# Rows of each expert loaded in parts of 16·m partitions, and one load of columns issued from another queue

## The chip, the core and the metric

One core of one Trainium2 chip. The metric is the device time of one execution in microseconds (us); before the change it is 1216.14 us, the median of three runs (1215.63 to 1216.97). Engines are called PE (matmul), PEld (its weight load), DVE (vector), ACT (scalar), POOL (GpSimd) and SP (the engine that here only issues transfers). About 2.4 us, 0.2% of the time, is what a measurement of this kernel can tell from no change.

## The reference

Three layers follow each other: attention that keeps the 32 largest scores of a row, a mixture of eight experts of which each token takes one, and a dense two-layer network.

```python
def _attn_ref(q, k, v):                       # 4 x 8 x 576 x 64
    scores = scale * np.matmul(q, k.transpose(0, 1, 3, 2))
    kth = np.partition(scores, -top_k, axis=-1)[..., -top_k:-top_k + 1]
    scores = np.where(scores >= kth, scores, -1000000000.0)
    ...
def _moe_ref(x, expert_emb, tau, w1, w2):     # 2304 tokens of 512, 8 experts, 1024 hidden
    expert_idx = np.argmax(logits, axis=1)
    for e in range(E):
        mask = expert_idx == e
        h = np.maximum(x[mask] @ w1[e], 0.0)
        out[mask] = gate_w[mask, None] * (h @ w2[e])
def _moe2_ref(x, w_in, w_out, alpha):         # 512 -> 2048 -> 512
    h = x @ w_in
    g = np.maximum(h, 0.0) + alpha * np.minimum(h, 0.0)
    return g @ w_out
```

## The kernel before

The attention runs to about 515 us. While it ends, the router finds the expert of each token and scatters the tokens' rows into the DRAM array `xs`, one region of 2304 rows for each expert; a row has 512 values, the token's number and its gate. The experts are then sorted by their number of tokens. The largest is rank 0, and each rank has a fixed number of columns that it computes: `CAPS`, 472, 408, 360, 328, 304, 296, 280 and 256.

`Experts.run` works on nine blocks: the first 216 tokens of rank 0 (`FIRST`, partly computed ahead, under the attention), its other 256, and ranks 1 to 7. A block of n tokens is a first product and a second product, 96 matmuls each. In the first product (lines 989 to 991) eight hidden tiles are computed, each twelve matmuls of n columns, into one of six PSUM banks (`mm`); ACT takes each out with a Relu (L1082) and DVE computes the low half (L1083). In the second product four output tiles (`dc` 0 to 3) are computed, 24 matmuls each. Tiles 0 and 2 are taken out by DVE (L1127), tiles 1 and 3 by ACT (L1125), into `y`, which has two buffers in all; from there SP stores them to the DRAM array `yt` (L1128), two ticks later. So tile 3 can be taken out only once the store of tile 1 has landed, and tile 2 once that of tile 0 has.

The rows of a block are loaded by `load_rows` (L957) into the tile `xr`, which has one buffer. Such a load is issued in the second product of the block two before, as soon as the rows that stood there have been transposed. A load of n rows is cut into nj parts of p partitions, where nj is the smallest of 1 to 4 that divides n into parts of at most 128: 216 is 2 x 108, 256 is 2 x 128, 408 is 4 x 102, 360 is 3 x 120, 328 is 4 x 82, 304 is 4 x 76, 296 is 4 x 74, 280 is 4 x 70. ACT multiplies each part by the gates (L973), in the first product of the block before the one that the rows are for. PE transposes the rows in four chunks, one matmul for each part and chunk (L981), in the second product of that same block; ACT and DVE take the chunks out (L983, L984). Four ticks after its load, `load_rows` also has the tokens' numbers copied from `xs` to the DRAM list `idc` (L964); for the first block it is done at once and from the tile (L967).

Weights are loaded on SP's queue too (L849 for the experts, L894 for the last network), converted by ACT (L923) and by DVE or POOL (L924), in the order in which `tick` meets them. All engines work in the order in which this code is written; SP's queue has the loads of rows, of weights and the stores of results, one behind the other.

After the experts, `last_products` runs the dense network in groups of 256 tokens. Its columns come back from `yt` through `load_columns` (L1143), again into `xr`. The load of the first group is issued in the second product of rank 6, that of the second group at the start of the first group's products. A rank stores its whole number of columns at a place that is known only at run time, so the framework lets a load from `yt` wait for every store before it, and a store wait for every load before it, unless the two are declared independent.

Of the kernel before, what the change touches and what calls it, by code (L numbers as in the profile page):

```python
# [21 lines left out]
P = 128  # L22
# [408 lines left out]
NT = B * S  # L431
E, FF, FF2, DM = 8, 1024, 2048, H * D
# [14 lines left out]
G2 = 256  # L447
# [367 lines left out]
class Experts:  # L815
# [3 lines left out]
    def __init__(self, tc, w1, w2, w_in, w_out, wa, xp, ident, xs, yt, idc, yp, ro, out):  # L819
        self.tc, self.nc = tc, tc.nc  # L820
        self.w1, self.w2, self.w_in, self.w_out = w1, w2, w_in, w_out
        self.ident, self.xs, self.yt, self.idc, self.out = ident, xs, yt, idc, out
        self.ro, self.wa, self.xp, self.yp = ro, wa, xp, yp
        self.W, self.rv = {}, {}
        self.items, self.sent = [], 0
        self.h0, self.p0 = [], []

    def reg(self, ap, n):
        return self.nc.values_load(ap, engines=[mybir.EngineType.SP], min_val=0, max_val=n,
# [102 lines left out]
    def after(self, n, f):  # L932

        self.stores.append((self.step + n, f))

    def tick(self, at, of):

        self.step += 1
        for x in [x for x in self.stores if x[0] <= self.step]:
            self.stores.remove(x)  # L940
            x[1]()
        k = (at + 1) * self.n // of - at * self.n // of if at >= 0 else 0
        for _ in range(k):
            if self.done == self.sent:
                self.send(1)
            self.items[self.done][1]()
            self.done += 1
            self.send(self.done + 3 - self.sent)

    def load_rows(self, r, o, n):  # L950

        nc = self.nc
        nj = next(j for j in (1, 2, 3, 4) if n % j == 0 and n // j <= P)
        p = n // nj
        e, base = self.rv[r]
        x = self.xp.tile([P, 4, XW], F32, name="xr")
        ld = nc.sync.dma_start(x[:p, :nj], self.xs[ds(e * NT + o, n)].rearrange("(j p) d -> p j d", p=p))  # L957
        if r == 0 and o == 0:
            assert len(self.ro.scat) == (B - 1) * BT
            self.ro.early = ld  # L960
        ids = self.idc[ds(base + o, n)] if r else self.idc[o:o + n]
        if r or o:
            src = self.xs[ds(e * NT + o, n), DM]
            self.after(4, lambda: nc.sync.dma_start(ids.rearrange("(a b) -> a b", a=8),  # L964
                                                    src.rearrange("(a b) -> a b", a=8)))
        else:
            nc.sync.dma_start(ids.rearrange("(j p) -> p j", p=p), x[:p, :nj, DM])  # L967
        return x, p, nj

    def gate(self, rows, j):  # L970
# [67 lines left out]
    def run(self, ctx, alpha):  # L1038
        tc, nc = self.tc, self.nc
        self.wb = ctx.enter_context(tc.tile_pool(name="wb", bufs=1, reuse_waits="tile"))  # L1040
        self.wk = ctx.enter_context(tc.tile_pool(name="moe", bufs=1, reuse_waits="tile"))
        self.ps = ctx.enter_context(tc.tile_pool(name="moe_ps", bufs=1, space=PSUM, reuse_waits="tile"))
        self.V, self.done, self.step, self.stores = {}, 0, 0, []
        blocks = [(0, 0, FIRST), (0, FIRST, CAPS[0] - FIRST)] + [(r, 0, CAPS[r]) for r in range(1, E)]
        units = lambda r, i: [self.plain(k) for k in range(8 * r + 4 * i, 8 * r + 4 * i + 4) if EARLY <= k < 8 * E]

        plan = [units(0, 1), [], units(1, 0), units(1, 1)]
        for r in range(1, E):
            plan += [units(r + 1, 0), units(r + 1, 1)]
        plan[-2] += [self.last(u) for u in range(4)]  # L1050
        plan[-1] += [self.last(u) for u in range(4, 8)]
        plan.append([self.wide(u, i) for u in range(STAY, 16) for i in range(2)])
        wide = [self.wide(u, i) for u in range(STAY) for i in range(2)]
        n = len(wide)
        first, m = WIDE
        for i in range(m):
            p = plan[first + i]
            at = lambda i: i if i == 0 else 4 + (n - 4) * (i - 1) // (m - 1)
            new = wide[at(i):at(i + 1)]
            plan[first + i] = [x for y in zip(p[:len(new)], new) for x in y] + p[len(new):] + new[len(p):]  # L1060
        self.wf = self.wb.tile([P, STAY, 1024], F32, name="wf")
        self.items = [x for p in plan for x in p]
        self.send(4)
        rki = self.ro.rki
        ranks = self.ro.ranks()

        def registers():
            for r in range(1, E):
                self.rv[r] = (self.reg(rki[0:1, 0, r:r + 1], E - 1), self.reg(rki[0:1, 1, r:r + 1], NT))
        self.alpha = self.wk.tile([P, FF2 // P], F32, name="alpha")  # L1070
        nc.sync.dma_start(self.alpha, alpha.rearrange("(f p) -> p f", p=P))
        xT = self.x0
        for i, (r, o, n) in enumerate(blocks):
            nb = blocks[i + 1] if i + 1 < len(blocks) else None
            hT, nx = ([] if i else self.h0), []
            self.n = len(plan[2 * i])
            for f in range(8):
                if i or f >= AHEAD:
                    ps = self.bank()[:, :n]
                    self.hidden(r, f, xT, ps)  # L1080
                    h = self.hidden_tile(f, [P, 2, MAXN])
                    nc.scalar.activation(h[:, 0, :n], ps, AF.Relu)  # L1082
                    nc.vector.scalar_tensor_tensor(h[:, 1, :n], ps, 0.0, h[:, 0, :n].bitcast(F32), op0=OP.max,  # L1083
                                                   op1=OP.subtract)
                    hT.append(h)
                if i == 0:
                    k = RANKS[f]
                    for step in ranks[:k]:
                        step()
                    ranks = ranks[k:]  # L1090
                    if len(ranks) < 14 and 1 not in self.rv:
                        registers()
                        rows = [self.load_rows(*nb)]
                if f >= GAT and nb and i:
                    self.gate(rows[0], f - GAT)
                if i:
                    self.tick(f, 8)
                else:
                    self.tick(SPLIT0.index(f) if f in SPLIT0 else -1, len(SPLIT0))
            if not nb:  # L1100
                nx = self.halves(rows[0])
            if i == 1:
                fl = self.flags()
            if i == 2:
                self.redo(*fl)
            base = self.rv[r][1]
            self.n = len(plan[2 * i + 1])

            def turn(at):
                if nb:  # L1110
                    nx.extend([self.x_chunk(rows[0], nb[2], d) for d in (XAT if i else XAT0)[at]])
                    if len(nx) == 4 and len(rows) == 1:
                        rows.append(self.load_rows(*blocks[i + 2]) if i + 2 < len(blocks) else self.load_columns(0))
            for dc in range(4):
                ps = self.bank()[:, :n]
                for f in range(8):
                    u = self.W[8 * r + 4 + f // 2]
                    c = slice((f % 2) * 512 + dc * P, (f % 2) * 512 + (dc + 1) * P)
                    self.mm3(ps, u[:, 0, c], u[:, 1, c], hT[f][:, 0, :n], hT[f][:, 1, :n], f == 0, f == 7)
                    if f == 3:  # L1120
                        self.tick(2 * dc, 8)
                        turn(2 * dc)
                y = self.wk.tile([P, 512], F32, name="y", bufs=2)
                if dc % 2:
                    nc.scalar.activation(y[:, :n], ps, AF.Copy)  # L1125
                else:
                    nc.vector.tensor_copy(y[:, :n], ps)  # L1127
                self.after(2, lambda r=r, o=o, n=n, dc=dc, y=y, base=base: nc.sync.dma_start(  # L1128
                    self.yt[dc, :, ds(base + o, n)] if r else self.yt[dc, :, o:o + n], y[:, :n]))
                self.tick(2 * dc + 1, 8)  # L1130
                if nb:
                    if i == 0 and dc == GAT0:
                        for j in range(4):
                            self.gate(rows[0], j)
                    turn(2 * dc + 1)
            xT, rows = nx, rows[1:]
        self.last_products(xT, len(plan[-1]))

    def load_columns(self, g):

        x = self.xp.tile([P, 4, XW], F32, name="xr")
        if g * G2 < NT:
            self.nc.sync.dma_start(x[:, :, :G2], self.yt[:, :, g * G2:(g + 1) * G2].rearrange("c p t -> p c t"))  # L1143
        return x

    def halves(self, x):
# [461 lines left out]
```

## Time and profile before

| what | us |
|---|---|
| median of three runs | 1216.14 |
| the profiled execution's own time | 1218.64 |
| its span, first to last instruction | 1216.8 |
| attention and router | 0 to about 525 |
| blocks of the experts | about 525 to 791 |
| dense network | 791 to 1216.8 |
| PE busy in the span | 1171.7 (96%) |

The span is read by stages: PE is at work nearly everywhere, so a change is worth what it gives back of the time in which PE waits, or of the matmuls themselves. The blocks of the experts can be told apart in the trace by the number of columns of their matmuls (128x408, 128x360 and so on), and the first product from the second by what is multiplied (`xT` or `hT`).

### The profile page before, as it was taken

To read this page: it belongs to the slowest core of one execution; us is meant where nothing else is said; L and a number is where in the kernel's file an instruction comes from. 1 tells how busy PE (TensorE), PEld (TensorE's weight loads), DVE (VectorE), ACT (ScalarE), POOL (GpSimd) and SP (SyncE) were. 2 spreads that over 40 slices of the span, in tenths; PEclk is the share of its full clock that TensorE was granted. 3 is DMA by queue.
4 is the path that set the end of the run, shared out by engine and by line. 5 is a ranking of instruction groups with operands and counts; after the bars stand their busy time and mean duration, and the time that the engine had idled before them with its cause. 6 is when DMAs were issued, how large, how long until landed. Compare 5 with 4: busy or idle time off the path is not lost.

```text
span 1216.8 us, 23815 instructions
## 1 busy us (share of the span) xinstructions
PE 1171.7 (96%) x7729; PEld 1028.1 (84%) x7729; DVE 871.8 (72%) x3629; ACT 695.0 (57%) x1495; POOL 725.6 (60%) x684
## 2 busy tenths in 40 slices
PE   7999999999999999998999899989999999999996
PEld 4778788778877886998999899978898998998995
DVE  5999999999999999776545376666657564454440
ACT  5899999999999998834434355422323222122120
POOL 4899988998999888743334255445345352333331
PEclk9999999999999999888999999989999999999998
DMA  5343222322231103168757688442232212212211
GB/s 132 100 114 109 61 53 56 91 62 55 57 91 37 33 13 132 30 159 223 202 160 197 177 241 236 126 113 70 78 113 70 65 58 70 78 62 78 72 43 55
DMA packets 121538, 120.85 MB, mean 99 GB/s; under 512 B 73380, under 2 KB 91300, under 8 KB 121404
## 3 DMA queue, kind: packets, MB, share of 16 engines
q1 hardware_dynamic: 118492, 109.78, 32.5%
q0 software_dynamic: 2912, 9.46, 2.2%
q8 instruction: 63, 1.03, 0.4%
q14 instruction: 71, 0.58, 0.2%
HBM read 84.25 MB, written 33.92 MB: 97 GB/s over the span
## 4 chain that ended last, share of the span: by engine, by line
PE 72%; DVE 12%; DMA 5%; ACT 3%; POOL 3%; issue 3%; SPq 1%; POOLq 0%; ACTq 0%; DVEq 0%
PE mm L990 10%; PE mm L991 10%; PE mm L989 10%; PE po L310 9%; PE s L165 8%; PE mm L1207 6%; PE mm L1206 6%; PE mm L1205 6%; PE pt L289 4%; DMA yt<-y 4%; DVE cand L186 3%; DVE mg L218 2%; DVE w L208 2%; POOL pm L269 2%; PE pt L145 1%
## 5 line engine op out<-in xcount | busy, mean ns | idle before, releaser
L989 PE MATMUL mm<-xT,wt 128*128 128x256 f32 (+7 forms) x852 | 249.2, 292 | 9.4 <-ACT xT L1150 5.5
L990 PE MATMUL mm<-xT,wt 128*128 128x256 f32 (+7 forms) x852 | 249.9, 293 | 4.3 <-DVE xT L984 4.2
L991 PE MATMUL mm<-xT,wt 128*128 128x256 f32 (+7 forms) x852 | 249.2, 292 | 0.0
L186 DVE MAX8 cand<-ss 128x8 f32<-128x82 f32 (+1 forms) x1008 | 231.7, 232 | 14.2 <-ACT ss L176 14.2
L263 POOL TENSOR_TENSOR z<-ss,sg 128x576 f32<-128x576 f32 x143 | 204.9, 1433 | 47.8 <-ACT sg L252 27.4
L310 PEld LDWEIGHTS po<-vt,pT 116*128 116x128 f32 x1440 | 175.8, 192 | 34.2 <-issue 23.9
L269 POOL TENSOR_TENSOR pm<-e,mg 128x576 f32<-128x576 f32 x141 | 199.1, 1412 | 2.7 <-ACT mg L243 2.2
L310 PE MATMUL po<-vt,pT 116*128 116x130 f32 x1440 | 197.2, 283 | 1.2 <-ACT pc L342 1.0
L1190 POOL TENSOR_TENSOR hT<-xr,hT 128x256 fp32r<-128x256 f32 x144 | 106.3, 743 | 153.3 <-ACT hT L1189 145.7
L1189 ACT ACTIVATE hT<-xr 128x256 fp32r<-128x256 f32 x144 | 59.1, 417 | 200.8 <-DVE xr L1186 194.0
L989 PEld LDWEIGHTS mm<-xT,wt 128*128 128x128 f32 x852 | 163.8, 192 | 11.6 <-ACT xT L1150 5.8
L165 PE MATMUL s<-qk 64*128 64x288 f32 x512 | 166.3, 447 | 3.8 <-ACT ss L176 3.2
L990 PEld LDWEIGHTS mm<-xT,wt 128*128 128x128 f32 x852 | 164.1, 193 | 5.4 <-DVE xT L984 4.4
L991 PEld LDWEIGHTS mm<-xT,wt 128*128 128x128 f32 x852 | 164.8, 193 | 0.0
L924 POOL TENSOR_TENSOR wt<-raw,wt 128x1024 fp32r<-128x1024 f32 x29 | 78.0, 2693 | 91.4 <-ACT wt L923 89.4
L1185 DVE TENSOR_SCALAR xr<-mm,alpha 128x256 f32<-128x256 f32 x144 | 69.3, 481 | 85.2 <-PE mm L991 84.3
L165 PEld LDWEIGHTS s<-qk 64*128 64x128 f32 x512 | 89.6, 194 | 43.7 <-issue 12.5
L252 ACT ACTIVATE sg<-ss,w 128x576 f32<-128x576 f32 x144 | 112.6, 782 | 5.2 <-DVE w L199 5.1
L176 ACT ACTIVATE ss<-s 128x576 f32<-128x576 f32 x144 | 94.9, 659 | 30.2 <-PE s L165 29.4
L257 ACT ACTIVATE e<-ss,sm 128x576 f32<-128x576 f32 x144 | 111.7, 776 | 0.0
L289 PE MATMUL pt<-ident,pm 128*116 128x128 f32 x720 | 105.4, 278 | 6.5 <-POOL pm L269 6.4
L208 DVE MAX8 w<-z 128x8 f32<-128x576 f32 x144 | 106.7, 741 | 2.5 <-POOL z L263 2.4
(249 smaller groups left out, 2493.6 us busy)
## 6 DMA issues: line engine op xcount, KB each, us to landing
raw<-in_moe_w SPq DMA_DIRECT2D x60, 512.0 KB
xr<-yt SPq DMA_DIRECT2D x18, 512.0 KB
xs<-zeros SPq DMA_DIRECT2D x8, 1028.0 KB
raw<-in_moe_w_in SPq DMA_DIRECT2D x16, 512.0 KB
raw<-in_moe_w_out SPq DMA_DIRECT2D x16, 512.0 KB
yt<-zeros SPq DMA_DIRECT2D x8, 704.0 KB
rows<-in_q SPq DMA_DIRECT2D x32, 144.0 KB
rows<-in_k SPq DMA_DIRECT2D x32, 144.0 KB
```

The source lines that it names most:

```text
L165: nc.tensor.matmul(s[:, g, :HALF], qs, t["qk"][hs, S + g * HALF:S + (g + 1) * HALF], start=True, stop=True)
L186: blocks.append(lambda i=i: nc.vector.max(A.cand[:, i], A.ss[:, i * BW:(i + 1) * BW if i + 1 < KB else S]))
L208: fin = [lambda: nc.vector.max(C.w[:, 24:32], C.z), lambda: nc.vector.scalar_tensor_tensor(scr, self.vsel, C.c1, C.w[:, 23:32, None].to_br ...
L252: nc.scalar.activation(T.sg, T.ss, AF.Sign, bias=T.w[:, 23:24], scale=-ABOVE, accum_out=T.c1)
L257: nc.scalar.activation(T.e, T.ss, AF.Exp, bias=T.sm[:, 0:1], scale=0.125)
L263: eng.tensor_tensor(T.z, T.ss, T.sg, op=OP.mult)
L269: eng.tensor_tensor(thirds(T.pm[:, :S]), thirds(T.e), T.mg, op=OP.mult)
L289: nc.tensor.transpose(o, T.pm[:, c * CK:(c + 1) * CK], self.ident)
L310: nc.tensor.matmul(po[:, i:i + 2, :], T.pT[:, c], rhs, start=(c == 0), stop=(c == NCK - 1))
L989: nc.tensor.matmul(ps, wh, xh, start=first, stop=False)
L990: nc.tensor.matmul(ps, wh, xl, start=False, stop=False)
L991: nc.tensor.matmul(ps, wl, xh, start=False, stop=last)
```

## The change

Two edits. In `load_rows` the parts have a multiple of 16 partitions: nj is n over 128, rounded up, and p is the smallest multiple of 16 with which nj parts hold n rows. 216 becomes 2 x 112, 408 4 x 112, 360 3 x 128, 328, 304 and 296 3 x 112, 280 3 x 96; 256 stays 2 x 128. The load then reads 8 to 40 rows more than the block has (none for 256), which lie in the same region of `xs`, and whose transposed columns nobody reads. The first block's numbers are stored part by part, two transfers for one, since its last part is not full. In `load_columns` the first call issues on ACT's queue, the others on SP's as before, and that load and the stores of ranks 2 to 7 are declared independent of each other (`put`, `behind`, `ahead_of`): the first 256 columns belong to rank 0.

```diff
--- before.py
+++ after.py
@@ -823,7 +823,7 @@
         self.ro, self.wa, self.xp, self.yp = ro, wa, xp, yp
         self.W, self.rv = {}, {}
         self.items, self.sent = [], 0
-        self.h0, self.p0 = [], []
+        self.h0, self.p0, self.behind, self.ahead_of = [], [], [], []
 
     def reg(self, ap, n):
         return self.nc.values_load(ap, engines=[mybir.EngineType.SP], min_val=0, max_val=n,
@@ -932,6 +932,14 @@
     def after(self, n, f):
 
         self.stores.append((self.step + n, f))
+
+    def put(self, r, st):
+
+
+        if r > 1:
+            self.behind.append(st)
+            for ld in self.ahead_of:
+                self.tc.declare_no_dep(st.ins, ld.ins, reason="columns of other tokens")
 
     def tick(self, at, of):
 
@@ -950,11 +958,11 @@
     def load_rows(self, r, o, n):
 
         nc = self.nc
-        nj = next(j for j in (1, 2, 3, 4) if n % j == 0 and n // j <= P)
-        p = n // nj
+        nj = -(-n // P)
+        p = -(-n // (16 * nj)) * 16
         e, base = self.rv[r]
         x = self.xp.tile([P, 4, XW], F32, name="xr")
-        ld = nc.sync.dma_start(x[:p, :nj], self.xs[ds(e * NT + o, n)].rearrange("(j p) d -> p j d", p=p))
+        ld = nc.sync.dma_start(x[:p, :nj], self.xs[ds(e * NT + o, p * nj)].rearrange("(j p) d -> p j d", p=p))
         if r == 0 and o == 0:
             assert len(self.ro.scat) == (B - 1) * BT
             self.ro.early = ld
@@ -964,7 +972,9 @@
             self.after(4, lambda: nc.sync.dma_start(ids.rearrange("(a b) -> a b", a=8),
                                                     src.rearrange("(a b) -> a b", a=8)))
         else:
-            nc.sync.dma_start(ids.rearrange("(j p) -> p j", p=p), x[:p, :nj, DM])
+            for j in range(nj):
+                m = min(p, n - j * p)
+                nc.sync.dma_start(self.idc[j * p:j * p + m], x[:m, j, DM])
         return x, p, nj
 
     def gate(self, rows, j):
@@ -1125,8 +1135,8 @@
                     nc.scalar.activation(y[:, :n], ps, AF.Copy)
                 else:
                     nc.vector.tensor_copy(y[:, :n], ps)
-                self.after(2, lambda r=r, o=o, n=n, dc=dc, y=y, base=base: nc.sync.dma_start(
-                    self.yt[dc, :, ds(base + o, n)] if r else self.yt[dc, :, o:o + n], y[:, :n]))
+                self.after(2, lambda r=r, o=o, n=n, dc=dc, y=y, base=base: self.put(r, nc.sync.dma_start(
+                    self.yt[dc, :, ds(base + o, n)] if r else self.yt[dc, :, o:o + n], y[:, :n])))
                 self.tick(2 * dc + 1, 8)
                 if nb:
                     if i == 0 and dc == GAT0:
@@ -1140,7 +1150,12 @@
 
         x = self.xp.tile([P, 4, XW], F32, name="xr")
         if g * G2 < NT:
-            self.nc.sync.dma_start(x[:, :, :G2], self.yt[:, :, g * G2:(g + 1) * G2].rearrange("c p t -> p c t"))
+            eng = self.nc.scalar if not self.ahead_of else self.nc.sync
+            ld = eng.dma_start(x[:, :, :G2], self.yt[:, :, g * G2:(g + 1) * G2].rearrange("c p t -> p c t"))
+            if not self.ahead_of:
+                self.ahead_of.append(ld)
+                for st in self.behind:
+                    self.tc.declare_no_dep(ld.ins, st.ins, reason="columns of other tokens")
         return x
 
     def halves(self, x):
```

SP's queue in the second product of rank 1, where the rows of rank 3 are loaded; `xr<-xs` is the load (partitions x parts x values), `yt<-y` the stores of output tiles 0, 1 and 2, `raw` weights. Before:

```order
L1128 DMA yt<-y 128x408
L849 ISA
L849 DMA raw<-in_moe_w 128x2x512
L957 ISA
L957 DMA xr<-xs 82x4x514
L1128 ISA
L1128 DMA yt<-y 128x408
L849 ISA
L849 DMA raw<-in_moe_w 128x1024
```

After:

```order
L1138 DMA yt<-y 128x408
L849 ISA
L849 DMA raw<-in_moe_w 128x2x512
L965 ISA
L965 DMA xr<-xs 112x3x514
L1138 ISA
L1138 DMA yt<-y 128x408
L849 ISA
L849 DMA raw<-in_moe_w 128x1024
```

Nothing moves: the load stands in the same place, with the store of tile 1 right behind it, and has three parts of 112 partitions for four of 82.

ACT's queue in the second product of rank 6, where the first columns for the dense network are loaded; `xT<-xt` takes out the transposed chunks of rank 7, `y<-mm` the output tiles 1 and 3, `hT<-mm` the hidden tiles of rank 7. Before:

```order
L923 ACTIVATE wt<-raw 128x1024 x2
L983 ACTIVATE xT<-xt 128x256 x2
L1125 ACTIVATE y<-mm 128x280
L983 ACTIVATE xT<-xt 128x256 x2
L923 ACTIVATE wt<-raw 128x1024 x2
L1125 ACTIVATE y<-mm 128x280
```

After:

```order
L923 ACTIVATE wt<-raw 128x1024 x2
L993 ACTIVATE xT<-xt 128x256 x2
L1135 ACTIVATE y<-mm 128x280
L993 ACTIVATE xT<-xt 128x256 x2
L1154 DMA xr<-yt 128x4x256
L923 ACTIVATE wt<-raw 128x1024 x2
L1135 ACTIVATE y<-mm 128x280
```

The load stands on ACT between the last chunks of rank 7 and two weight conversions. On SP, at the same place, it is gone from between a weight load and the store of tile 1. Before:

```order
L849 DMA raw<-in_moe_w 128x2x512
L1143 DMA xr<-yt 128x4x256
L1128 ISA
L1128 DMA yt<-y 128x280
L1128 ISA
```

After:

```order
L849 DMA raw<-in_moe_w 128x2x512
L1138 ISA
L1138 DMA yt<-y 128x280
L1138 ISA
L1138 DMA yt<-y 128x280
```

The stores of tiles 1 and 2 of rank 6 no longer stand behind a load; the order of the others is as it was. On ACT four multiplications by the gates are gone (one part less in ranks 3 to 6), and on PE sixteen transposes.

## Rows read from the trace of the kernel before

**Rows 1.** The page, part 1: busy us, share of the span, instructions.
```profile
PE 1171.7 (96%) x7729; PEld 1028.1 (84%) x7729; DVE 871.8 (72%) x3629; ACT 695.0 (57%) x1495; POOL 725.6 (60%) x684
```

**Rows 2.** Waits of PE from 500 us on: waiting <- releaser, us, times, longest.
```profile
PE mm L989 <- ACT xT L1150: 5.5, 1, 5.5
PE mm L990 <- DVE xT L984: 4.2, 1, 4.2
PE mm L989 <- ACT y L1125: 3.2, 2, 3.0
```

**Rows 3.** PE by stage: stretch, us, busy (instructions), granted clock, DMA share, GB/s.
```profile
596.20:615.37 19.17, 19.17 (x110) 1.00 0.41 136
615.37:632.30 16.93, 16.32 (x97) 1.00 0.70 171
632.30:650.75 18.45, 17.21 (x113) 1.00 0.83 241
650.75:665.25 14.50, 14.50 (x98) 1.00 0.62 167
665.25:681.50 16.25, 15.79 (x114) 1.00 0.60 198
681.50:700.02 18.52, 15.28 (x98) 0.91 0.67 150
700.02:715.51 15.49, 14.81 (x114) 1.00 0.76 246
...
728.53:742.71 14.18, 14.18 (x115) 1.00 0.81 277
...
768.33:779.63 11.30, 11.30 (x98) 1.00 0.17 55
694.40:697.80 3.40, 3.12 (x13) 0.50 0.40 120
```

**Rows 4.** Timeline of ACT, output tile 3: start, us, form, [idle before <- releaser].
```profile
625.04 0.51 ACT L1125 ACTIVATE y<-mm 128x408 f32<-128x408 f32 x1 [15.83 <-DMA yt<-y]
657.57 0.47 ACT L1125 ACTIVATE y<-mm 128x360 f32<-128x360 f32 x1 [12.00 <-DMA yt<-y]
692.50 0.45 ACT L1125 ACTIVATE y<-mm 128x328 f32<-128x328 f32 x1 [15.54 <-DMA yt<-y]
718.05 0.42 ACT L1125 ACTIVATE y<-mm 128x304 f32<-128x304 f32 x1 [5.70 <-DMA yt<-y]
742.95 0.42 ACT L1125 ACTIVATE y<-mm 128x296 f32<-128x296 f32 x1 [3.38 <-PE mm L991]
```

**Rows 5.** The chain that ended last, from 600 us: start, us, what.
```profile
607.11 17.82 DMA yt<-y
```

**Rows 6.** Timeline of SP: start, us taken by issuing.
```profile
675.38 6.84 SPq L1128 DMA_DIRECT2D yt<-y  x1
```

**Rows 7.** Transposes on PE by shape, 535:765 us: count, busy us, mean ns.
```profile
L981 PE MATMUL xt<-ident,xr 102*128 102x102 f32 x16 | 1.7, 250 | 0.0
L981 PE MATMUL xt<-ident,xr 120*128 120x120 f32 x12 | 1.6, 265 | 0.0
L981 PE MATMUL xt<-ident,xr 82*128 82x82 f32 x16 | 1.5, 234 | 0.0
```

**Rows 8.** Timelines of SP (first column load) and of ACT behind it.
```profile
765.64 0.38 SPq L1143 DMA_DIRECT2D xr<-yt  x1
...
771.42 0.40 ACT L1125 ACTIVATE y<-mm 128x280 f32<-128x280 f32 x1 [5.10 <-PE mm L991]
```

**Rows 9.** Waits of SP's queue from 760 to 772 us: us, times, longest.
```profile
SPq L1128 <- DMA xr<-yt: 3.3, 1, 3.3
SPq L1143 <- DMA yt<-y: 3.0, 1, 3.0
```

**Rows 10.** Timeline at the second group's columns: ACT takes them, PE goes on.
```profile
807.73 1.32 ACT L1150 ACTIVATE xT<-xr 128x256 fp32r<-128x256 f32 x4
...
808.18 0.58 PE L989 MATMUL mm<-xT,wt 128*128 128x256 f32 x1 [5.54 <-ACT xT L1150]
```

## The prediction

> **What bounds the kernel now.** I read four views, from the whole to the part. The page's first lines [rows 1] show PE at work for 96% of the span, so what the change can give back lies in the remaining 4% or in the matmuls. PE's waits from 500 us on [rows 2] come to few: 5.5 us for `xT` of the dense network, 4.2 us for an `xT` of the first blocks, 3.2 us for ACT's `y`, and some smaller ones behind DVE. The busy times by stage [rows 3] place the third. The product stages of the experts run at a steady price for each column where nothing disturbs them: in a first product 14.50 us for 328 columns and 11.30 us for 256, both 0.0441 us a column; in a second product, transposes included, 19.17 us for 408 and 14.18 us for 296, that is 0.0470 and 0.0479, middle 0.0474. Against these prices five stages are too long:
>
> - 615.37, rank 2 first, 360 columns: 16.93 against 15.88, 1.05 us over
> - 632.30, rank 2 second, 360: 18.45 against 17.08, 1.37 over
> - 665.25, rank 3 second, 328: 16.25 against 15.56, 0.69 over
> - 681.50, rank 4 first, 304: 18.52 against 13.41, 5.11 over
> - 700.02, rank 4 second, 304: 15.49 against 14.42, 1.07 over
>
> Together 9.3 us. Part of the 5.11 is the clock: after PE had waited, the granted clock was 0.50, the lower level of 1.2 GHz, from 694.40 to 697.80 [rows 3], where 13 matmuls ran in 3.40 us instead of some 24 (13.41 us over 96 is 0.14 us each), a loss of 1.5 us.
>
> The cause stands on ACT [rows 4]. Before it can take out output tile 3, ACT waits for the store of tile 1, since `y` has two buffers: 15.83 us in the stage from 615.37, 12.00 us in that from 650.75, 15.54 us in that from 681.50. While ACT stands there, PE fills the free banks and then stops. The chain that ended last runs through the store: 17.82 us from issue to landing [rows 5]. In front of that store SP had issued the rows of the rank two further on, in four parts of 82 partitions; in the other two long waits they had 76 and 74. Where the load in front had parts of 70, the wait is 5.70 us, and where they were 128 ACT waits for PE instead [rows 4]; the stage between these two, 728.53, is busy throughout [rows 3]. A store took 6.84 us only to be issued [rows 6], so the queue behind such a load was full. The size doesn't sort the waits (4 x 74 rows are fewer than 4 x 76, and the wait is longer), the number of parts doesn't (70 comes in four parts too): the number of partitions does.
>
> The Trainium skill has a rule for it (DMA: Bandwidth & Descriptors, section "Why a DMA increments its semaphore by 16 and not by 1"): a transfer runs on the largest number of DMA engines, at most 16, that divides the slowest dimension. That makes 2 engines of 82 and of 74, 4 of 76, 14 of 70 and 16 of 128; the waits of ACT stand in just that order. By it all loads of the changed kernel, of 112 and 96 partitions too, run on 16, and the sum would be the one below, with the first rival left out.
>
> **The change part by part.** *The loads.* No load of before has 112 or 96 parts. The nearest rows are 128 (no wait for the store) and 70 (5.70 us) on the good side, 76 (12.00 us) on the bad one. I take the good side, since 112 and 96 are 16 times 7 and 6 as 128 is 16 times 8. With a wait of at most 5.70 us nothing of the five excesses remains: 9.3 us gained, 0 lost. What is late next is then ACT's own reading of tile 3 after PE has finished it, as in the row at 742.95, and PE waits for nobody there. Should the good side fail, the price at 12.00 us is the stage pair of rank 3: nothing over in the first product (14.50 us, busy throughout), 0.69 us in the second.
>
> *The transposes.* Sixteen fewer, but of more columns. By [rows 7] one costs 1.7/16 = 0.106 us at 102, 1.6/12 = 0.133 at 120, 1.5/16 = 0.094 at 82, so about 0.12 at 112, 0.14 at 128 and 0.10 at 96. Rank 1: 16 at 112 for 16 at 102, +0.2 us. Rank 2: 12 at 128 for 12 at 120, +0.1. Ranks 3 to 6: 12 each for 16 each, 1.4 and 1.2 us for 1.5 to 1.3, about 0. The sum is +0.3 us, all on PE. Bounds: -1.6 us if a transpose cost the same at any width (16 at 0.1), +0.8 if it went by columns alone.
>
> *The gates.* Four multiplications fewer on ACT, no cost, and no gain, for ACT waits in these stages.
>
> *The first block's numbers.* One issue more on SP, 0.4 us by the like row [rows 8], under the attention's last products; nobody waits for the list before the end of the experts. 0.
>
> *The column load.* Before, SP's queue stood 3.0 us until the last store had landed, issued the load, and the next store stood 3.3 us more behind it [rows 9]; ACT got to tile 3 of rank 6 only at 771.42 [rows 8]. PE lost nothing by it: from 768.33 to 779.63 it is busy for 11.30 of 11.30 us [rows 3]. So these 6.3 us of the queue go, and the gain is 0, covered by PE's five free banks. Now the instruction stands in ACT's queue behind the chunks of rank 7, whose transposes are what it needs; behind it wait two weight conversions and tile 3. Its price on ACT lies between 0.38 us, SP's own issue [rows 8], and 6.84 us, the longest issue seen [rows 6]. I take 0.4, as the queue is new and empty. Either is hidden: ACT was held up to 771.42 before and PE did not stop. 0.
>
> The Trainium skill speaks against a gain here (the same page, section "Issuing engines are not separate DMA queues"): issuing from several engines saves only the sequencer's time, the transfers share the same engines. By it this edit could give at most the 6.3 us of SP's queue, by the rows 0; the trace here agrees that the queue was the only thing held.
>
> *The sum.* -9.3 + 0.3 = -9.0 us. The profiled execution took 1218.64 us (span 1216.8 us, 1.8 us around it), 2.5 us over the median; for it the sum makes 1209.6 us, and on the median 1216.14 it makes 1207.1 us.
>
> **Rivals.**
>
> *112 parts behave like 76.* ACT then waits some 12 us in the three stages. Of the 15.54 us wait in rank 4's first product PE stood 3.0 us (the longest of its waits for `y` [rows 2]), so its cover there is about 12.5 us and 12.00 just fits. What is left is the 0.69 us of rank 3 in each of the three ranks: gain 9.3 - 2.1 = 7.2, time 1209.3. Against it: 70 parts, even more irregular, waited 5.70.
>
> *The parts don't matter.* If the bytes of these stages, 167 to 246 GB/s [rows 3], make the stores late, nothing but the transposes changes: 1216.4. Against it: the stage from 728.53 has the same or more.
>
> *It gives more.* One may hope that the load free of the stores also ends PE's longest wait, 5.54 us before the second group [rows 10]; with the slower clock after it this would make 1207.1 - 5.5 - about 1.5, some 1200. Against it: ACT's `xT` at 807.73 has no idle time of its own in the row, the columns are those of the second load, which stays on SP, and DVE and ACT come to it through their conversions.
>
> *Slower: ACT stuck at its new load.* The place is ACT's queue at about 763 us. If the instruction waits there, the Relus behind it wait, and PE goes on until its banks are full: tile 3 is finished at about 768.3, and five hidden tiles of 12 matmuls (11.30/8 = 1.41 us each) later, at 775.4, PE stops. So from a wait of about 12 us on each us costs one, and 9.0 + 2.4 us must be eaten before the kernel is slower by what can be told: some 23 us, for 1219 us. The longest issue seen is 6.84 us, the longest landing 17.82; and nothing that it waits for is late. Improbable.
>
> **How the numbers follow.** Forecast 1207.1 us, chance 0.72; 112 like 76 (1209.3) 0.09; parts without effect (1216.4) 0.08; more (1200) 0.08; slower (1219) 0.03. The forecast's own width: the transposes -1.6 to +0.8 instead of +0.3, the second products' prices between 0.0470 and 0.0479 (0.9 us over 992 columns), a tenth of the gain left behind in small waits, and 1 us between medians: 1204 to 1210. Taking in the first rival and half of what could come beyond on either side, the range is 1203.5 to 1211.5. Faster by over 0.2%: 0.72 + 0.09 + 0.08 = 0.89. Within 0.2% (2.4 us, what this measurement can tell): 0.08. Slower: 0.03.
>
> **What would show it.** In the new profile: ACT's wait for `y`'s store before tile 3 is under 6 us in all ranks; no issue on SP takes over 2 us behind a row load; the first product of 304 columns takes 13.4 us and that of 360 15.9, at the full clock; SP's waits around the first column load are gone and PE is still busy throughout there; the 5.5 us wait before the second group stands. The prediction is wrong if ACT's waits stay over 12 us, if they shrink and PE stops elsewhere in the same stages (then most likely at a weight, which ACT takes in order), or if the wait before the second group moves.

## The result and the profile after

The changed kernel takes 1207.5 us, the median of six runs (1204.66 to 1208.03); the kernel before, in six runs, takes 1216.55 (1214.25 to 1218.84). The ratio is 0.9914, with a 95% interval of 0.9899 to 0.9928: faster, by 0.7 to 1.0%. Predicted were 1207.1 us.

The first part of the page of the changed kernel (busy us, share of the span, instructions), the line to put beside [rows 1]:

```profile
PE 1164.7 (97%) x7713; PEld 1022.6 (85%) x7713; DVE 869.2 (72%) x3629; ACT 695.7 (58%) x1491; POOL 723.2 (60%) x684
```

PE is busy 7.0 us less, in a span that is 12.7 us shorter. The waits of PE from 500 us on (waiting, releaser, us, times, longest), against [rows 2]:

```profile
PE mm L999 <- ACT xT L1165: 5.5, 1, 5.5
PE mm L1000 <- DVE xT L994: 4.4, 1, 4.4
...
PE xt L991 <- DVE xT L994: 0.9, 2, 0.6
```

The wait for ACT's `y` is gone; the two for `xT` stand as they were. PE by stage (stretch, us, busy, granted clock, DMA share, GB/s), against [rows 3]; the first six are rank 2 first and second, rank 3 first and second, rank 4 first and second, the seventh is the first product of rank 7:

```profile
612.98:628.76 15.78, 15.78 (x97) 1.00 0.72 144
628.76:645.64 16.88, 16.88 (x110) 1.00 0.79 253
645.64:660.14 14.50, 14.50 (x98) 1.00 0.76 148
660.14:675.72 15.58, 15.58 (x110) 1.00 0.83 270
675.72:689.11 13.39, 13.39 (x99) 1.00 0.83 134
689.11:703.72 14.61, 14.61 (x111) 1.00 0.86 281
...
756.46:767.76 11.30, 11.30 (x98) 1.00 0.04 14
```

Each stage is busy from end to end at the full clock. Against [rows 3] the five long ones lose 1.15, 1.57, 0.67, 5.13 and 0.88 us, 9.40 together; rank 3 first and rank 7 first, which were not too long before, take what they took. The GB/s of these stages moved both ways (171 to 144 in rank 2 first, 198 to 270 in rank 3 second): the bytes were not what was in the way.

The cause on ACT, output tile 3 in the timeline (start, us, form, idle before and its releaser), against [rows 4]:

```profile
613.23 0.51 ACT L1135 ACTIVATE y<-mm 128x408 f32<-128x408 f32 x1 [6.45 <-PE mm L1001]
...
675.97 0.45 ACT L1135 ACTIVATE y<-mm 128x328 f32<-128x328 f32 x1 [4.82 <-PE mm L1001]
...
704.54 0.42 ACT L1135 ACTIVATE y<-mm 128x304 f32<-128x304 f32 x1 [4.94 <-DMA yt<-y]
```

Where 15.83, 12.00 and 15.54 us ended with the store of `y`, ACT now waits for PE (5.41 us in the row left out), which is no loss: it is there before the tile is. Of the rows shown only the last, behind a load of 96 partitions, still ends with the store, after 4.94 us. On SP, the store behind the row load of rank 3 in the kernel before, that of [rows 5] (start, us taken by issuing):

```profile
607.11 6.72 SPq L1128 DMA_DIRECT2D yt<-y  x1
```

and the row load and the store behind it at the same place in the changed kernel:

```profile
604.25 0.34 SPq L965 DMA_DIRECT2D xr<-xs  x1
604.79 0.38 SPq L1138 DMA_DIRECT2D yt<-y  x1
```

The store is issued in 0.38 us, where it took 6.72 (the 6.84 of [rows 6] are those behind the load of 74 partitions), and in the trace it lands 5.0 us later, where it took 17.82.

The column load in ACT's queue, with the conversions behind it, the place of [rows 8]:

```profile
750.50 0.44 ACTq L1154 DMA_DIRECT2D xr<-yt  x1
...
750.99 2.14 ACT L923 ACTIVATE wt<-raw 128x1024 fp32r<-128x1024 f32 x2
756.70 0.40 ACT L1135 ACTIVATE y<-mm 128x280 f32<-128x280 f32 x1 [3.58 <-PE mm L1001]
```

It takes 0.44 us of ACT, and ACT is back in time for tile 3.

Of the 12.7 us of span, the profiles put 9.9 into the blocks of the experts (264.34 to 254.48 us from the first product to the dense network), 2.0 ahead of them and 0.8 behind, with the same instructions on PE there. The two last parts are not laid to the change: in the kernels below, which share the code of the attention, the first product starts anywhere from 524.1 to 527.7 us.

### The profile page after: what moved, and what is told of

The parts are those of the page before. It is cut to its first block, busy times and chain, and to the rows that moved or that the text cites. A ratio compares the mean times of both kernels' runs of the same rounds, so it can differ in the third digit from the quotient of the medians.

```text
span 1204.1 us, 23779 instructions
## 1 busy us (share of the span) xinstructions
PE 1164.7 (97%) x7713; PEld 1022.6 (85%) x7713; DVE 869.2 (72%) x3629; ACT 695.7 (58%) x1491; POOL 723.2 (60%) x684
## 4 chain that ended last, share of the span: by engine, by line
PE 83%; DVE 8%; ACT 3%; POOL 2%; issue 2%; DMA 1%; POOLq 0%; SPq 0%; DVEq 0%; ACTq 0%
PE mm L1000 12%; PE mm L1001 12%; PE mm L999 12%; PE po L310 10%; PE s L165 10%; PE mm L1222 6%; PE mm L1221 6%; PE mm L1220 6%; PE pt L289 5%; DVE cand L186 2%; PE pt L145 2%; DVE mg L218 1%; POOL pm L269 1%; DVE w L208 1%; DMA yt<-y 1%
```

## The experiments

The theory: a load of rows whose parts have a poor number of partitions is slow, the queue of SP fills behind it, and the store of tile 1 comes late. The rivals: the gain is the column load's; it is the smaller number of parts or transposes; it is only the store's place behind the load. Ratios are to the kernel before, run on the same chip.

**One edit at a time.** The first kernel has the parts alone, with `load_columns` as before; the second has the column load on ACT's queue alone, with the parts as before. Their cores, against the changed kernel:

```diff
-            eng = self.nc.scalar if not self.ahead_of else self.nc.sync
-            ld = eng.dma_start(x[:, :, :G2], ...)
+            self.nc.sync.dma_start(x[:, :, :G2], ...)
```

```diff
-        nj = -(-n // P)
-        p = -(-n // (16 * nj)) * 16
+        nj = next(j for j in (1, 2, 3, 4) if n % j == 0 and n // j <= P)
+        p = n // nj
```

> The kernel before with the loads in parts of 16m partitions alone; the first columns still come from SP's queue. My theory (the gain is the row loads' and nothing else): 1207.5 us, ratio 0.991 to 0.993, PE's busy stages as in the changed kernel. Rival (the load on ACT's queue brings part of it, by freeing SP's queue for 6.3 us): over 1209.5 us.

> The kernel before with the first column load on ACT's queue and free of the stores of ranks 2 to 7, the row loads as before. My theory: no change, 1216.5 us, ratio 0.999 to 1.001; SP's two waits of 3.0 and 3.3 us around that load are gone, ACT takes out tile 3 of rank 6 some 3 us earlier than 771.42, and PE is as busy as before there. Rival (it is worth something by itself): 1214 us or less.

Measured: 1208.63 us, ratio 0.9911 (0.9890 to 0.9932) for the parts, 1219.84 us, ratio 1.0003 (0.9991 to 1.0015) for the column load. PE's rank 4 first with the column load alone:

```profile
679.53:698.52 18.99, 15.20 (x98) 0.91 0.65 138
```

The excess of [rows 3] is there, 18.99 us against 13.39, and so are those of the other stages (17.01 us in rank 2 first, 15.90 in rank 4 second). With the parts alone they are gone (15.79, 13.39 and 14.61 us in the three), although SP's queue still stands around the column load as in [rows 9], 2.3 us ahead of it and 3.8 behind it (waits of SP in the kernel with the parts alone, 740 to 780 us):

```profile
SPq L1130 <- DMA xr<-yt: 3.8, 1, 3.8
```

With the column load alone SP's two waits are gone, as expected, but ACT did not take out tile 3 of rank 6 some 3 us earlier: it came to it 2.29 us after the end of the stage (769.55 against 767.26), where it had been 3.09, since it then stood 3.81 us for the store of tile 1. PE was busy throughout either way. So the whole gain is that of the parts, and 6.1 us of a standing queue at the column load are worth nothing.

**Which numbers of partitions.** Two kernels are the changed one but for one line, which gives ranks 3 to 5 three parts of 122 or of 116 partitions. They have as many parts and transposes as the changed kernel, and more rows than it.

```diff
         p = -(-n // (16 * nj)) * 16
+        p = 122 if r in (3, 4, 5) else p      # the other kernel: 116
```

> The changed kernel, but the rows of ranks 3, 4 and 5 in three parts of 122 partitions instead of 112. As many parts and 9% more bytes. My theory (the number of partitions decides, by its divisors; 122 is 2 x 61): ACT again waits some 15 us for the store before tile 3 in the three stages, and the time goes back to 1215 to 1219 us. Rival (fewer parts or fewer instructions made the gain): 1207 to 1209 us.

> The changed kernel, but the rows of ranks 3, 4 and 5 in three parts of 116 partitions (4 x 29), which stands to the others as 76 did. My theory: ACT waits some 12 us for the store, which PE's free banks just cover, so only the catching up afterwards costs, 0.7 us in each of three ranks: 1209 to 1211 us, between the changed kernel and that with parts of 122. Rival (every part that isn't a multiple of 16 costs alike): as with 122, 1215 us or more.

Measured: 1234.22 us, ratio 1.0123 (1.0098 to 1.0147) with 122; 1212.74 us, ratio 0.9938 (0.9914 to 0.9963) with 116. ACT's tile 3 with 122 partitions, behind the first two of the three loads (18.95 us behind the third):

```profile
628.69 0.51 ACT L1136 ACTIVATE y<-mm 128x408 f32<-128x408 f32 x1 [18.20 <-DMA yt<-y]
...
669.06 0.47 ACT L1136 ACTIVATE y<-mm 128x360 f32<-128x360 f32 x1 [20.26 <-DMA yt<-y]
```

and with 116, behind the last two (11.82 us behind the first):

```profile
655.40 0.47 ACT L1136 ACTIVATE y<-mm 128x360 f32<-128x360 f32 x1 [12.00 <-DMA yt<-y]
...
685.84 0.44 ACT L1136 ACTIVATE y<-mm 128x328 f32<-128x328 f32 x1 [10.98 <-DMA yt<-y]
```

Neither the number of parts nor of transposes can do this. 116 waits as 76 did (12.00 us, [rows 4]) and 122 as 82 and 74 did or longer. The Trainium skill (DMA: Bandwidth & Descriptors, section "Why a DMA increments its semaphore by 16 and not by 1") gives 122 two DMA engines, 116 four and 112 sixteen. The trace agrees, with waits for the store of 18 to 20 us behind 122, 11 to 12 behind 116, and none behind 112 in the changed kernel, where PE is later than the store. (In the two kernels below that hold ACT, one wait behind 112 ended with the store, after 5.36 and 7.03 us; PE lost nothing by it, with 13.39 us for rank 4 first in both.)

The trace also records each transfer's completions one by one, and there the numbers can be counted. Besides one record right after the issue, the row loads have two completions with 82, 74 and 122 partitions, four with 76 and 116, fourteen with 70; with 112, 128 and 96 they have sixteen and no early one. The store behind the load has sixteen in every case, and they split in the same way. In the kernel before, the load of 82 partitions, issued at 606.64, completed at 623.88 and 624.20; of the store issued at 607.11, fourteen completions came by 615.75 and the last two at 624.92 and 624.93. Behind the load of 76, twelve came within 3.93 us of the store's issue and the last four after 13.06 to 13.93, right behind the load's four. In the changed kernel all sixteen came 4.38 to 5.0 us after the issue. So the store did not stand behind the load as a whole: as many of its sixteen shares as the load had late completions came behind the load, the others went ahead, and ACT needs all sixteen.

With 122 I had expected a loss of less than half that size. Two things were missed. A load of 366 rows on two engines is longer than one of 328 or 296 (19.5 to 22.4 us from issue to landing in the trace, against 17.55 and 17.41), and rank 4's load, four parts of 76 before, joined the slow ones. The cover, the time for which PE goes on with the banks that are still free, does not grow with the load: in ACT's waits of 18.20, 20.26 and 18.95 us PE stopped for 2.52, 6.36 and 6.32, so 15.7, 13.9 and 12.6 us were covered, less with fewer columns. What lies beyond shows on PE, and the clock with it (PE in the first product of rank 3, and the stretch behind its stop):

```profile
654.00:677.69 23.69, 17.33 (x97) 0.86 0.58 155
...
668.50:675.30 6.80, 5.72 (x21) 0.50 0.41 129
```

23.69 us stand against 14.50 in the changed kernel (and 22.08 against 13.39 in rank 4); after the stop PE runs at 0.50, the level of 1.2 GHz, for 6.80 us.

With 116 the first products are undisturbed and only the second ones are a little long (ranks 3, 4 and 5):

```profile
663.08:679.45 16.37, 15.90 (x111) 1.00 0.79 248
...
692.83:709.01 16.18, 14.92 (x110) 1.00 0.77 237
...
722.03:736.51 14.48, 14.38 (x110) 1.00 0.82 273
```

Against the changed kernel (15.58, 14.61 and 14.09) that is 0.79, 1.57 and 0.39 us, 2.75 in all. This is the first rival of the prediction, acted out: it was priced at 2.1 us of loss. The ratio 0.9938 is 0.24% behind 0.9914, 2.9 us, but the two intervals overlap; it is the stages that show the difference.

**Is it the store's place behind the load?** In the kernel before, the stores of `y` are issued one tick earlier (a tick is one step of the code's own schedule, two for each output tile), so that the store of tile 1 stands in front of the row load.

```diff
-                self.after(2, lambda ...: nc.sync.dma_start(self.yt[...], y[:, :n]))
+                self.after(1, lambda ...: nc.sync.dma_start(self.yt[...], y[:, :n]))
```

> The kernel before, row loads as they were (82, 76, 74 partitions), but each output tile is stored one tick earlier, so that the store of tile 1 stands ahead of the row load on SP's queue instead of behind it. My theory (the slow load hurts by the store queued behind it, for which ACT waits): ACT's waits of 12 to 16 us before tile 3 fall under 6 us although the loads are as slow as before, and most of the 9 us come back: ratio 0.992 to 0.996. Rival (it hurts as much by the weights queued behind it, or by taking two DMA engines from everything): ratio 0.998 or more.

Measured: 1225.27 us, ratio 1.0053 (1.0035 to 1.0072), slower than the kernel before. My expectation failed, and usefully; the time is that of the rival. The store does what was hoped; ACT's tile 3 behind the loads of 82 and 74 partitions, and of 76 too, waits for PE:

```profile
615.01 0.51 ACT L1125 ACTIVATE y<-mm 128x408 f32<-128x408 f32 x1 [6.41 <-PE mm L991]
...
684.76 0.45 ACT L1125 ACTIVATE y<-mm 128x328 f32<-128x328 f32 x1 [4.78 <-PE mm L991]
```

But the wait has moved to the next thing in the queue. PE in the second product of rank 2 and both of rank 4, and the row of ACT behind the load of 82 partitions:

```profile
630.55:653.62 23.07, 20.03 (x114) 0.85 0.67 204
684.51:697.90 13.39, 13.39 (x99) 1.00 0.67 148
697.90:717.71 19.81, 17.12 (x114) 0.91 0.74 220
```

```profile
627.86 1.06 ACT L923 ACTIVATE wt<-raw 128x1024 fp32r<-128x1024 f32 x1 [8.48 <-DMA raw<-in_moe_w]
```

The first products are as short as in the changed kernel (6.3 us gained in ranks 2 and 4), and the second ones lose more than that: 23.07 and 19.81 us against 18.45 and 15.49 in [rows 3], 8.9 us. (The second products of ranks 5 and 6 and of rank 0's other 256 tokens lose another 1.80, 4.16 and 4.04 us; what makes these was not followed up.) ACT, in order, stands at a weight for 8.48 us with the Relus behind it. What this run cannot say alone is whether the slow load holds the weights, or the earlier store itself, at which SP stands until `y` is written while weights queue behind.

So the same line was put into the changed kernel, whose loads are fast.

> The changed kernel, parts of a multiple of 16 partitions, with the stores of y issued one tick earlier, as in e6_store_before_load. It tells apart what made that run slower. Theory: the slow load held the weights queued behind it; here the loads are fast, so the earlier place costs next to nothing: ratio to the kernel before 0.990 to 0.993, second products of ranks 2 to 6 within 0.5 us of those of the changed kernel (16.88, 15.58, 14.61, 14.09, 13.21). Rival: the earlier place costs by itself, since SP stands in order at each store until y is written, and the weights behind it are issued later; then most of the loss of that run is here too: ratio 0.998 to 1.005, and second products of 17 to 23 us.

Measured: 1208.79 us, ratio 0.9898 (0.9879 to 0.9918), not to be told from the changed kernel. The second products of ranks 2, 4 and 5:

```profile
627.64:644.51 16.87, 16.87 (x109) 1.00 0.74 203
687.98:702.92 14.94, 14.88 (x111) 1.00 0.80 245
...
715.93:731.55 15.62, 14.93 (x110) 1.00 0.79 255
```

Rank 2 takes 16.87 us against 23.07, rank 4 14.94 against 19.81: with the store at the same place in the queue, 6.2 and 4.9 us hang on the load alone. The earlier place has a small price too (rank 5 is 1.53 us over the changed kernel and rank 6, with 14.54 us, 1.33, more than the half I had allowed); the first blocks give it back, with 14.11 us for 17.55 in the stage where PE waits for `xT`. ACT's waits for weights from 600 to 780 us, in the changed kernel, in the one with the store earlier, and in the one before with the store earlier, show the two parts:

```profile
ACT wt L923 <- DMA raw<-in_moe_w: 2.0, 4, 0.7
```

```profile
ACT wt L923 <- DMA raw<-in_moe_w: 19.5, 10, 3.3
```

```profile
ACT wt L923 <- DMA raw<-in_moe_w: 36.7, 15, 8.5
```

What is shown, then: the slow load delays what is issued behind it, store or weight, and taking one of them out of its shadow puts the next one there. The completions say the same of a weight: in the kernel before, of the one issued at 614.08, behind the load of 82 partitions, fourteen came by 618.82 and the last two at 627.15 and 627.46. All these transfers were issued on SP's queue. Whether a row load or a store on another queue would escape was not tried, and stays open.

**How long may ACT be held at the column load?** The prediction's slower rival was ACT stuck at its new load. Here ACT copies 128 x 1024 values right behind it, 8 times in one kernel and 20 times in the other, into a part of `xr` that nobody reads.

```diff
             if not self.ahead_of:
+                for _ in range(8):      # the other kernel: 20
+                    self.nc.scalar.activation(x[:, :, G2:2 * G2], self.wf[:, 0].rearrange(...), AF.Copy)
                 self.ahead_of.append(ld)
```

> The changed kernel with 8 extra copies of 128x1024 on ACT (about 1.06 us each, 8.5 us) right behind the load on its queue; their result is not used. By the price that the prediction gave for a held ACT (PE's free banks cover some 12 us there): no change against the changed kernel, 0.9914 of before. Rival (ACT's place there is on the path): +4 us or more, over 0.994.

> As the one before with 20 copies, 21 us. By the same price PE stops for 21 + 2 x 1.06 for the conversions behind them, less the cover: 9 to 12 us, and 1.5 to 3 us for the clock: 10 to 15 us over the changed kernel, ratio 1.000 to 1.004 of before. Rival (the cover is larger, as more than banks can give way): under 5 us over the changed kernel.

Measured: ratio 0.9920 (0.9902 to 0.9937) with 8 copies, nothing that can be told from the changed kernel; 1.0043 (1.0024 to 1.0062) with 20. ACT with 20 copies (the load, the copies, the conversions, tile 3):

```profile
754.82 0.44 ACTq L1154 DMA_DIRECT2D xr<-yt  x1
...
755.30 21.80 ACT L1157 ACTIVATE xr<-wf 128x1024 f32<-128x1024 f32 x20
777.01 1.99 ACT L923 ACTIVATE wt<-raw 128x1024 fp32r<-128x1024 f32 x2
778.91 0.38 ACT L1135 ACTIVATE y<-mm 128x280 f32<-128x280 f32 x1
```

and PE, stopped until then (its timeline, and the granted clock from within the stop on):

```profile
779.34 0.58 PE L999 MATMUL mm<-xT,wt 128*128 128x256 f32 x1 [12.75 <-ACT y L1135]
```

```profile
770.90:784.50 13.60, 5.16 (x24) 0.50 0.07 23
```

PE stopped at 766.59, 11.8 us after the load was issued. Of a hold of 21.80 us 12.75 became a stop, so 9.05 were covered. The first product of rank 7 took 26.65 us instead of 11.30: 15.35 lost, a little over the 10 to 15 expected: 12.75 by the stop and 2.6 behind it, nearly all by PE at the level of 1.2 GHz (24 matmuls took 5.16 us; at 11.30 us for 96 they take 2.8).

**What else could be had.** Two waits of PE are left, 5.5 us before the second group and 4.4 us in the first blocks (3.6 to 5.7 in the other kernels that keep its cause). In the next kernel the weights that ACT converts in the first group come at other ticks, none of them ahead of the second group's columns.

```diff
-                self.tick(g * 8 + f if h == 0 else -1, ng * 8)
+                self.tick((g - 1) * 8 + f if h == 0 and g else -1, (ng - 1) * 8)
```

> The changed kernel, but the conversions of w_out and w_in that the dense network spreads over its first nine groups are spread over the eight after the first. The prediction said that the 5.5 us wait of PE before the second group is made by DVE's and ACT's conversions and not by the columns. By that it falls to about 1 to 1.5 us, and the slower clock after it goes: 5 to 7 us under the changed kernel, ratio 0.986 to 0.988 of before. Rival (the wait is for the columns or for the products themselves): as the changed kernel, 0.991.

Measured: 1204.01 us, ratio 0.9871 (0.9853 to 0.9888). PE's waits from 520 to 800 us:

```profile
PE mm L1000 <- DVE xT L994: 5.5, 1, 5.5
PE mm L999 <- ACT xT L1165: 1.9, 1, 1.9
```

The wait before the second group is 1.9 us instead of 5.5. The last kernel takes the other one too, with one buffer `y` shared by two output tiles where a block has at most 256 columns.

```diff
-                y = self.wk.tile([P, 512], F32, name="y", bufs=2)
+                if n > 256 or dc % 2 == 0:
+                    y = y2 = self.wk.tile([P, 512], F32, name="y", bufs=2)
+                else:
+                    y = y2[:, 256:]
```

> The changed kernel with the tick of the run e9_no_conversion_first_group (no weight conversion before the second group) and, in blocks of at most 256 tokens, one buffer y held by two output tiles, so that tile 2 no longer waits for the store of tile 0. Theory: in the first blocks DVE stands at tile 2 until tile 0's store has landed, so it comes late to the last xT, and PE waits 4.4 to 5.5 us for it at about 550 us, with a slower clock behind it. Without that wait 4 to 6 us go beside the 4 of e9: ratio to the kernel before 0.982 to 0.984. Rival: DVE is late by its own work there, or waits for something else; then the wait of over 4 us stands and the ratio is that of e9, 0.987.

Measured: 1202.45 us, ratio 0.9846 (0.9826 to 0.9865), the best of all. The waits of PE from 500 us on:

```profile
PE xt L991 <- DVE xT L994: 2.4, 2, 1.3
...
PE mm L1000 <- DVE xT L994: 0.6, 1, 0.6
```

The cause was named rightly: with the store out of DVE's way the wait of 5.5 us is 0.6. The gain is smaller than expected, some 3 us by the ratios, whose intervals overlap. The stage where PE waited fell from 17.55 us in the changed kernel to 12.30, but the one after it grew from 13.48 to 15.21, as PE now waits for the `xT` chunks of the next block (2.4 us against 0.9). One profile is a rough measure here: the first of the two stages took 17.55 to 19.97 us in the kernels that have the stores and `y` as before.

## Why the prediction was right, point by point

*The five stages.* Predicted excesses 1.05, 1.37, 0.69, 5.11 and 1.07 us, 9.3 together; measured 1.15, 1.57, 0.67, 5.13 and 0.88, 9.40, the changed transposes of these stages included. The prices for a column held: 15.78 us for 360 columns against 15.88, 13.39 for 304 against 13.41. That all of the excess would go, and no other wait step in, was the choice with the most weight, and the run with the store moved shows that it was not self-evident: there another wait did step in. It rested on the loads themselves becoming fast.

*112 on the good side.* Chosen by 128 and 70, against 76; the wait behind 112 ends with PE, and 116 shows how near the bad side lies. What sorts the loads is not their size but what divides the number of partitions.

*The full queue.* One step of the working was not right, without weight for the sum: the 6.84 us that a store took to be issued [rows 6] were read as a queue that such a load fills. Behind 76 partitions the store was issued in 0.57 us and still landed only after 13.93, and behind 82 fourteen of its sixteen completions came some 9 us before the last two. The store is late by the shares of it that come behind the load's, as the completions above show; the long issue is a second thing, seen only behind loads of 74, 82 and 122 partitions.

*The transposes.* Predicted +0.3 us on PE. The groups of the changed kernel by shape, 535 to 765 us (count, busy us, mean ns):

```profile
L991 PE MATMUL xt<-ident,xr 112*128 112x112 f32 x52 | 6.5, 261 | 0.2 <-DVE xT L994 0.2
L991 PE MATMUL xt<-ident,xr 128*128 128x128 f32 x28 | 4.3, 274 | 0.6 <-DVE xT L994 0.6
L991 PE MATMUL xt<-ident,xr 96*128 96x96 f32 x12 | 1.3, 245 | 0.0
```

That is 0.125, 0.154 and 0.108 us each, where 0.12, 0.14 and 0.10 were taken from [rows 7], and 12.1 us in all against 11.5 before: +0.6, within the bounds of -1.6 and +0.8.

*The gates and the first block's numbers.* No wait in the profile after shows either; 0 as predicted, though no run had one of them alone.

*The column load.* Predicted 0.4 us on ACT and no gain; 0.44 us, and a ratio of 1.0003 alone. The Trainium skill's rule that issuing from another engine saves only sequencer time (DMA: Bandwidth & Descriptors, section "Issuing engines are not separate DMA queues") agrees with it.

*The slower rival's price.* One term was off, without weight for the result. I had counted five free banks behind tile 3 and 7 us of products in them; PE stopped 5.8 us after the end of tile 3's product (766.59 against 760.77), that is four tiles. The cover from the load on, 11.8 us, came near the 12 named, but the two conversions and tile 3 stand in it too, so 9 us of a hold are free, not 12, and a hold of 21.80 us, where 23 were named, already makes the kernel slower.

*The sum.* -9.0 us predicted for the median, -9.05 measured between the medians of six runs; the ratio's interval makes it 8.8 to 12.3. So close a hit is partly luck: that interval is 3.5 us wide.

## What to carry to other kernels

Look at what the number of partitions of a transfer divides by before looking at its size: 112 partitions with rows that nobody reads beat 82, 76 or 74 exact ones (0.9914), 116 in the same three ranks gave back less (0.9938), and 122 was slower than the exact ones (1.0123). When an engine waits for a store, look at what was queued in front of the store; moving the store only handed the wait to the next transfer behind the slow one. And ending the stand of a queue gave nothing where the engine behind it had cover: cost the cover in tiles, with what else must run before the engine is free.

## What the runs showed of the hardware that was not expected

A load on few engines held up only a part of what was issued behind it, and its own row shows nothing wrong: with 122 partitions it was issued in 0.27 us, faster than the good ones (0.34). The row behind it can show it, as single stores there took 9.30 and 9.22 us to be issued (SP's timeline):

```profile
646.34 0.27 SPq L966 DMA_DIRECT2D xr<-xs  x1
646.80 9.30 SPq L1139 DMA_DIRECT2D yt<-y  x1
```

but it need not. Behind the load of 76 partitions, in the kernel before, the store was issued in 0.57:

```profile
643.53 0.57 SPq L1128 DMA_DIRECT2D yt<-y  x1
```

Both landed late, 22.15 and 13.93 us after their issue, although fourteen completions of the first had come within 10.97 us and twelve of the second within 3.93. So the landing is what has to be looked at. And a stop of PE cost more than its length: the 12.75 us behind ACT were followed by matmuls at 0.50 until 784.50, 2.6 us more on the stage.
